# Second product terms: exchanged by plain transfers and added on GpSimd, in place of accumulating transfers

## The chip, the cores and the metric

The kernel runs on one core of a Trainium2 chip. The metric is device time in microseconds (us) for one execution, the smaller the better. A core has engines that run side by side, each its own list of instructions in order: TensorE (PE, with its weight loads shown apart as PEld), VectorE (DVE), ScalarE (ACT), GpSimd (POOL) and SyncE (SP), whose work here is to issue transfers. Transfers (DMA) run on 16 shared DMA engines, from queues of their own: one is filled by SP, another by POOL.

## The reference

Two state-space convolutions of the same input are mixed by a gate. Input `u` is 2048 positions by 512 channels, the state has 128 terms for each channel:

```python
dt = jnp.exp(log_dt)
A = -jnp.exp(log_A_real) + 1j * A_imag
C = (C_real + 1j * C_imag) * dt[:, None]
P = jnp.exp((A * dt[:, None])[:, :, None] * pos[None, None, :])
K = 2.0 * jnp.einsum("dn,dnl->dl", C, P).real
y = jnp.fft.irfft(jnp.fft.rfft(u_t, 2 * L) * jnp.fft.rfft(K, 2 * L), 2 * L)[:, :, :L]
...
g = _sigmoid((x * gate_w).sum(-1, keepdims=True))
return g * a + (1 - g) * b        # a, b: y + u * D_skip with the weights A and B
```

## The kernel before

**Stages.** Parameters come in eight chunks of 128 channel rows and are prepared in five batches (`prep_ops`; the first on DVE, the other four on POOL, 25 steps each there). Each chunk is eight units, 64 in all. For one unit POOL multiplies two decay grids out of small bases (`grid0` writes 128x1024 numbers, `grid1` 128x512, both line 530), PE makes phases (`phase`), ACT turns them into sines and cosines, DVE multiplies them into the grids, and PE contracts the result into the convolution kernel's samples (`modes`, line 581). The grids have two buffers each, so POOL can run about two units ahead of `modes`. Four units make a block; there are 16.

**The transform of a block.** Kernel samples and inputs are transformed in two steps on PE (`first`, line 603; `s2`, line 640). The complex product of the two spectra is taken on DVE by `products` (line 651), which writes two terms: the first into the block's part of the tile `xall` (`xk(b)`; two such parts are used by turns), the second into `t2`, another part of `xall`, of which there is one. Real and imaginary parts lie on different halves of the 128 partitions, and the second term comes out on the opposite half. So the second has to cross over before the two can be summed. For 15 of the blocks `add_products` (line 681) does both at once: POOL issues four accumulating transfers per block, for two halves `h` of the columns and two halves `x` of the partitions, 256 KB each. `inverse` (line 694) then reads the sum on PE, its first two groups the columns of `h = 0`, its last two those of `h = 1`. For the last block no sum is made: `inverse` multiplies the second term by `mt`, which is the matrix `mi` with its row halves exchanged. `keep_z` stores the result; after every fourth block `final` multiplies by the gated synthesis matrix and `final_keep` and `final_out` write out.

**What sets the order.** All operations are listed in program order and then emitted in the order of the list `ORDER`; every engine keeps this order exactly, and so does SP's list of transfers. An instruction that must wait holds up everything behind it on its engine. `SLOTS` gives each PSUM tile one of eight banks.

**Tiles that the change touches.** `ks` (samples of a unit, four buffers), `ot` (outputs, four buffers), `mt`, `ident` (the identity; used by warm-up matmuls, by the preparation and by `hold`, idle filler matmuls) and `f1` (the smaller grid with its product).

Of the kernel before, what the change touches and what calls it, by code (L numbers as in the profile page):

```python
# [19 lines left out]
M = 32  # L20
# [185 lines left out]
def tile_gated_s4d(ctx: ExitStack, tc: tile.TileContext, nsb, a, out):  # L206
# [629 lines left out]
    def block(b):  # L836
# [9 lines left out]
        if 0 <= b < nblk - 1:  # L846
            for h in range(2):
                for x in range(2):
                    op("ya", add_products, b, h, x)
# [172 lines left out]
```

## Time and profile before

| | |
|---|---|
| Time, median of 3 runs (lowest, highest) | 500.42 us (500.07, 506.3) |
| The profiled execution: its own time | 500.83 us |
| its span, first to last instruction | 498.9 us |
| mean granted TensorE clock | 0.983 |
| busy in the span: PE, ACT, DVE, POOL | 443.1, 405.2, 392.9, 332.9 us |
| packets of SP's queue (q1) | 27360, 31.41 MB, 22.2% of 16 engines |
| packets of POOL's queue (q0) | 4800, 15.73 MB, 19.0% of 16 engines |

Busy time of an engine is the union of its instructions' spans; "idle before" is what an engine stood still ahead of an instruction, with the event that ended it. Matmuls are pipelined, so a busy PE isn't PE at its best.

### The profile page before, as it was taken

The page shows a single profiled execution, that of the slowest core. Times are in us where ns is not written, and L with a number is a line of the kernel's source. Part 1 is how long each engine was busy: PE and PEld are TensorE (multiplying, and loading weights), DVE is VectorE, ACT ScalarE, POOL GpSimd, SP SyncE. Part 2 cuts the span into 40 slices and gives each one's busy share as a digit, 9 for nine tenths or more (in the row PEclk, how much of TensorE's full clock was granted, in tenths as well). Part 3 has the DMA queues.
Part 4 walks back from the last instruction along what each step waited for, and adds up shares of the span by engine and source line. Part 5 has one row for each costly group of instructions (what it writes and reads, how often), then busy time and mean ns, then how long its engine had stood idle before and what let it go on. Part 6 is the DMA issues. An engine that isn't in the chain of part 4 may idle for free.

```text
span 498.9 us, 27908 instructions
## 1 busy us (share of the span) xinstructions
PE 443.1 (89%) x12448; PEld 357.4 (72%) x12448; DVE 392.9 (79%) x864; ACT 405.2 (81%) x816; POOL 332.9 (67%) x316
## 2 busy tenths in 40 slices
PE   5967997988999887997999898978998899989988
PEld 5855556876778675875888686767777779767984
DVE  6394898899999975888889795787999898976402
ACT  5697999989899987788998997777999797964323
POOL 1497998899997977686667866385775754862000
PEclk9998999999999999998999998999999999999999
DMA  4669705316550704246430744134443733174201
GB/s 143 226 235 287 186 11 126 69 25 123 136 94 12 150 27 98 69 77 157 79 61 11 150 105 74 57 78 96 113 77 60 157 65 67 36 169 74 59 25 60
DMA packets 32279, 48.92 MB, mean 98 GB/s; under 512 B 10144, under 2 KB 17440, under 8 KB 32160
## 3 DMA queue, kind: packets, MB, share of 16 engines
q1 hardware_dynamic: 27360, 31.41, 22.2%
q0 software_dynamic: 4800, 15.73, 19.0%
q8 instruction: 97, 1.59, 1.3%
q14 instruction: 22, 0.18, 0.1%
HBM read 17.25 MB, written 5.77 MB: 46 GB/s over the span
## 4 chain that ended last, share of the span: by engine, by line
PE 61%; ACT 12%; DVE 8%; issue 8%; POOL 7%; DMA 5%; SPq 0%; DVEq 0%; ACTq 0%; POOLq 0%
PE ps L640 15%; PE psi L694 11%; PE pk L581 9%; PE p0s L514 7%; PE ps L603 5%; DMA xall<-xall 5%; PE pf L718 4%; POOL f L530 3%; PE psu L603 3%; ACT bas L498 2%; ACT xall L610 2%; PE pw L289 2%; PE pw L293 2%; PE psg L782 1%; DVE xall L651 1%
## 5 line engine op out<-in xcount | busy, mean ns | idle before, releaser
L530 POOL TENSOR_TENSOR f<-bas 128x1024 f32<-128x1024 f32 (+1 forms) x128 | 207.7, 1689 | 78.6 <-PE pk L581 45.4
L640 PE MATMUL ps<-xall,gk 128*64 128x64 f32 (+1 forms) x1728 | 111.3, 251 | 5.7 <-DVE f L553 1.7
L640 PEld LDWEIGHTS ps<-xall,gk 128*64 128x64 f32 (+1 forms) x1728 | 101.4, 153 | 19.1 <-issue 2.7
L651 DVE TENSOR_TENSOR xall<-ps,v 128x256 f32<-128x256 f32 x256 | 94.5, 415 | 15.5 <-PE ps L640 13.4
L581 PE MATMUL pk<-f,f 128*32 128x64 f32 x4096 | 74.3, 223 | 15.5 <-issue 7.2
L581 PEld LDWEIGHTS pk<-f,f 128*32 128x32 f32 x4096 | 62.9, 111 | 27.6 <-issue 17.2
L694 PE MATMUL psi<-mi,xall 128*128 128x128 f32 x512 | 71.8, 287 | 4.4 <-issue 2.7
L681 POOL DMA_DIRECT2D xall<-xall x60 | 60.1, 1152 | 17.4 <-DVE f L557 8.1
L694 PEld LDWEIGHTS psi<-mi,xall 128*128 128x128 f32 x512 | 63.5, 196 | 10.2 <-issue 5.0
L557 DVE TENSOR_TENSOR f<-f,p0c 128x512 f32<-128x512 f32 x64 | 43.6, 682 | 14.4 <-ACT p0c L526 13.8
L514 PE MATMUL p1s<-cph,ones 64*128 64x512 f16 x128 | 49.3, 386 | 3.2 <-DVE ks L591 2.1
L553 DVE TENSOR_TENSOR f<-f,p0c 128x512 f32<-128x512 f32 x64 | 43.6, 681 | 8.6 <-ACT p0c L526 7.9
L603 PEld LDWEIGHTS ps<-w,ks 64*64 64x64 f32 x2048 | 35.4, 140 | 20.7 <-issue 7.7
L514 PE MATMUL p0s<-cph,ones 64*128 64x512 f16 x128 | 49.4, 386 | 0.5 <-ACT xall L610 0.4
L514 PE MATMUL p1s<-cph,rot 64*128 64x512 f16 x128 | 49.0, 382 | 0.8 <-issue 0.8
L569 DVE TENSOR_TENSOR f<-f,p1c 128x512 f32<-128x512 f32 x64 | 43.6, 682 | 7.3 <-ACT p1c L526 5.6
L610 ACT COPY xall<-ps 128x512 f32<-128x512 f32 x64 | 36.9, 612 | 15.0 <-PE ps L603 15.0
L603 PE MATMUL ps<-w,ks 64*64 64x64 f32 x2048 | 40.3, 227 | 9.6 <-issue 6.3
L514 PE MATMUL p0s<-cph,rot 64*128 64x512 f16 x128 | 48.9, 382 | 0.0
L701 ACT COPY z<-psi 128x512 f32<-128x512 f32 x64 | 37.9, 609 | 12.7 <-PE psi L694 12.7
L573 DVE TENSOR_TENSOR f<-f,p1s 128x512 f32<-128x512 f32 x64 | 43.6, 681 | 5.2 <-ACT p1s L523 4.1
L565 DVE SCALAR_TENSOR_TENSOR f<-f,p0s 128x512 f32<-128x512 f32 x64 | 43.4, 680 | 3.2 <-ACT p0s L523 3.0
(128 smaller groups left out, 824.1 us busy)
## 6 DMA issues: line engine op xcount, KB each, us to landing
xall<-xall POOLq DMA_DIRECT2D x60, 256.0 KB, 5.2
v<-v SPq DMA_DIRECT2D x64, 128.0 KB, 3.3
uraw<-in_us SPq DMA_DIRECT2D x16, 256.0 KB, 3.8
z<-in_ut SPq DMA_DIRECT2D x16, 256.0 KB, 6.4
out_dram<-ot SPq DMA_DIRECT2D x28, 128.0 KB, 2.2
par<-in_par SPq DMA_DIRECT2D x8, 256.0 KB, 4.4
gk<-in_gk SPq DMA_DIRECT2D x4, 512.0 KB, 6.1
eg<-in_eg SPq DMA_DIRECT2D x4, 512.0 KB, 5.6
```

Source lines behind the costliest of these rows:

```text
L514: PE.matmul(ps, w[h : h + 64], cph[h : h + 64, j], start=j == 0, stop=j == 3, tile_position=(h, 0))
L530: G.tensor_tensor(o.rearrange("p k (a b) -> p k a b", b=8), x[:, :, hi : hi + n].unsqueeze(3).to_broadcast([128, 16, n, 8]), x[:, :, lo : ...
L553: V.tensor_tensor(f0[:, 0, :, 0:32], f0[:, 1, :, 0:32], half(u, p0c[u], True), OP.mult)
L557: V.tensor_tensor(f0[:, 0, :, 32:64], f0[:, 1, :, 32:64], half(u, p0c[u], False), OP.mult)
L569: V.tensor_tensor(f[:, 0], f[:, 1], p1c[u], OP.mult)
L581: PE.matmul(pk[32 * kd : 32 * kd + 32, i, :], f1[:, p, 4 * i + kd, :], f0[:, p, 4 * i + kd, :], start=p == 1, stop=p == 0, tile_position=( ...
L603: PE.matmul(ps[h][64 * ri : 64 * ri + 64, n, :], x[r], w1[r, ri, r], start=True, stop=True, tile_position=(64 * h, 64 * ri),)
L610: S.copy(o, pxs[key][h])
L640: PE.matmul(ps[h : h + w, j, 0:n], gk[:, k, h : h + w], xall[:, x0:x1, 2 * k : 2 * k + 2], start=True, stop=True, tile_position=(0, h),)
L651: V.tensor_tensor(k.rearrange("p x (k t) -> p k x t", t=2), p2s[b, g][:, :, 0:64].rearrange("p k (x t) -> p k x t", t=2), vv.unsqueeze(3). ...
L681: G.dma_start(out=xk(b)[o, s], in_=t2[t, s], accum_op=OP.add)
L694: PE.matmul(ps[:, i, :], t[:, x : x + 2, :].rearrange("p x k -> p (x k)"), w, start=n == 0, stop=n == len(parts) - 1,)
```

## The change

The accumulating transfers go. For each block but the last and each column half, `exchange` has SP issue two plain transfers that copy the second term into the new tile `tx` with the partition halves exchanged, and `add_products` has POOL add `tx` to `xk(b)` in one 128x1024 instruction. `tx` has one buffer and holds one column half: the second half's exchange waits for the first half's add. That is 60 transfers of 256 KB on SP and 30 additions on POOL, for 60 transfers on POOL.

Room for `tx` (4 KB of each partition) comes from `mt` (its content is loaded over `ident` late in the run), from `ks` (three buffers, not four) and from `ot` (two, not four); the last outputs are gathered in a buffer of `f1`.

`ORDER` and `SLOTS` are new lists. On PE the units come in the same sequence with nearly the same work between them from unit 10 to unit 40; in the first units the gate matmuls (`ga`) stand earlier. On SP twelve, not three, of the 16 loads of `ut` stand ahead of the first load of `rot` (`turns`). On POOL the preparation of the third batch done there stands earlier. Counted in the two lists, after the memsets at the start POOL has this to do up to the last grid of unit 19, that grid included:

| | before | changed |
|---|---|---|
| grids | 40 | 40 |
| `amplitudes` | 3 | 3 |
| preparation steps (batches 1, 2, 3) | 25 + 25 + 8 | 25 + 25 + 23 |
| transfers issued | 12 | 0 |
| additions | 0 | 6 |

The fifteen additional preparation steps are nine TENSOR_TENSOR (128x256), five TENSOR_SCALAR (128x256) and one TENSOR_TENSOR of 128x768 (`rest`, line 406).

```diff
--- before.py
+++ after.py
@@ -31,173 +31,175 @@
 
 
 ORDER = [
...
 ]
 
 
 SLOTS = [
     int(c) for c in (
...
     )
 ]
 
@@ -238,10 +240,10 @@
     gk = const.tile([128, M, 128], F32, name="gk")
     dl = const.tile([128, 4 * nunit], F32, name="dl")
     mi = const.tile([128, 128], F32, name="mi")
-    mt = const.tile([128, 128], F32, name="mt")
     v = const.tile([128, 4, M, 32], F32, name="v")
     xall = const.tile([128, 128, 2 * M], F32, name="xall")
     t2 = xall[:, 32:64]
+    tx = const.tile([128, 16, 2 * M], F32, name="tx")
     z = const.tile([128, 128, 5 * NB], F32, name="z")
     eg = const.tile([128, 2, Q, M], F32, name="eg")
     warm = const.tile([128, 1], F32, name="warm")
@@ -584,7 +586,7 @@
                     )
 
     def keep(u):
-        kss[u] = work.tile([128, 4, Q], F32, name="ks", tag="ks", bufs=4)
+        kss[u] = work.tile([128, 4, Q], F32, name="ks", tag="ks", bufs=3)
         S.copy(kss[u], pks[u])
 
     def skip(u):
@@ -675,21 +677,26 @@
     def both_v(i, h):
         dma(v_at(hi, i, 0, h), v_at(lo, i, 0, h))
 
-    def add_products(b, h, x):
+
+    def exchange(b, h, x):
         o, t = slice(64 * x, 64 * x + 64), slice(64 - 64 * x, 128 - 64 * x)
-        s = slice(16 * h, 16 * h + 16)
-        G.dma_start(out=xk(b)[o, s], in_=t2[t, s], accum_op=OP.add)
+        dma(tx[o], t2[t, 16 * h : 16 * h + 16])
+
+    def add_products(b, h):
+        x = xk(b)[:, 16 * h : 16 * h + 16]
+        G.tensor_tensor(x, x, tx, OP.add)
 
     def z_place(b):
         sb, j = divmod(b, 4)
         return j if sb % 2 == 0 else 4 - j
+
 
 
     def inverse(b, g):
         pis[b, g] = ps = bank("psi", (128, 4, 128))
         for i in range(4):
             x = 2 * (4 * g + i)
-            parts = [(xk(b), mi), (t2, mt)] if b == nblk - 1 else [(xk(b), mi)]
+            parts = [(xk(b), mi), (t2, ident)] if b == nblk - 1 else [(xk(b), mi)]
             for n, (t, w) in enumerate(parts):
                 PE.matmul(
                     ps[:, i, :], t[:, x : x + 2, :].rearrange("p x k -> p (x k)"), w,
@@ -728,7 +735,7 @@
         return o[128 * i : 128 * (i + w)].rearrange("(p c) -> p c", p=128)
 
     def final_keep(sb, j, dp):
-        ots[sb, j, dp] = work.tile([128, 256], F32, name="ot", tag="ot", bufs=4)
+        ots[sb, j, dp] = work.tile([128, 256], F32, name="ot", tag="ot", bufs=2)
         w = 128 if sb == nsb - 1 else 256
         S.copy(ots[sb, j, dp][:, 0:w], pfs[sb, j, dp].rearrange("p a b -> p (a b)"))
 
@@ -755,7 +762,10 @@
         pfs[i] = ps
 
     def last_keep(i, dp):
-        ots[i, dp] = work.tile([128, 256], F32, name="ot", tag="ot", bufs=4)
+        if dp == 0:
+            f = work.tile([128, 2, 16, M], F32, name="f1", tag="f1").rearrange("p v k m -> p (v k m)")
+            for n in range(2):
+                ots[i, n] = f[:, 256 * n : 256 * n + 256]
         o = ots[i, dp].rearrange("p (a b) -> p a b", a=8)
         copy = V.tensor_copy if dp else S.copy
         for rq in range(4):
@@ -846,7 +856,8 @@
         if 0 <= b < nblk - 1:
             for h in range(2):
                 for x in range(2):
-                    op("ya", add_products, b, h, x)
+                    op("ya", exchange, b, h, x)
+                op("yb", add_products, b, h)
         if nxt:
             for h in range(2):
                 for i in range(2):
@@ -874,8 +885,6 @@
         op("ga", gate, j)
         op("gs", gate_sig, j)
         op("ge", gate_e, j)
-    for h in range(2):
-        op("lm", dma, mt[64 * h : 64 * h + 64], a["mi"][64 - 64 * h : 128 - 64 * h])
     for u in range(nunit):
         if u % 8 == 0:
             c = u // 8
@@ -885,6 +894,9 @@
                         batch(i)
                 chunk(c + 1)
         unit(u)
+        if u == nunit - 8:
+            for h in range(2):
+                op("lm", dma, ident[64 * h : 64 * h + 64], a["mi"][64 - 64 * h : 128 - 64 * h])
         b, n = divmod(u, 4)
         if b % 2 and n < 2 and b < nblk - 1:
             inputs(b + 1 + n)
```

More of the change, by code (lines that the diff above doesn't have):

```diff
@@ L192 @@
     int(c) for c in (
-        "012313131203231045671056710432305410726067134215247362064051571203517501406340652137625304"
-        "751046016231460173537512043672106723744160516743241726052657234605714531705426025471251746"
-        "301604352435041670362145125460173165726074265310253014215640372157146752350275604135231457"
-        "602670425352130264725065316205374134621357662074275436120162032176456204573134150261230572"
-        "546617045704521643125275071243624712341213246540752653121460154712543761016451675403142204"
-        "152637625074310775210471257625142675073320167540215437563412743145065260431773167502704512"
-        "726375607132164501754231762073463147065414140525417052461351276306740563130206314275140761"
-        "35064257370215170173041673152454325745314123521515"
+        "012312120131120450627642701246423670631452613672013260543146720564507350127350231657416307"
+        "243571206702557614306412641537014753624270641235412745670540346752617462754301570436324076"
+        "542140624057362167520143040153327612540341325062735026507561201437271403164257412630612304"
+        "275257147531056725436425017450261353640761532047162761325762732614056124132734620750265130"
+        "437621364310425640721024307271562156735267215420341475621465105730415652061052725130643163"
+        "245230471625402613402637415376412674012346013205273546104502617310247357531266050457364021"
+        "326045061475302315064760520617374026135012435676521241345705742645210363260540767524031452"
+        "60724043254757317135137562652741617232375112572171"
     )
```

310 rows, old and new, of the table ORDER are left out of this document.

## Prediction, made before the changed kernel was run

> **What bounds the kernel now.** I read the page first: which engine is full, and when.
>
> ```profile
> span 498.9 us, 27908 instructions
> ...
> PE 443.1 (89%) x12448; PEld 357.4 (72%) x12448; DVE 392.9 (79%) x864; ACT 405.2 (81%) x816; POOL 332.9 (67%) x316
> ...
> PE   5967997988999887997999898978998899989988
> ...
> POOL 1497998899997977686667866385775754862000
> ```
>
> PE has 89% of the span, so 55.8 us of it is idle and no change that leaves the matmuls alone can gain more than that. POOL looks harmless at 67%, but its row of slices is near full from the third to the twelfth and loose behind it. So the share has to be split by stage. The windows below run from the first base (18 us) to the end of unit 19's grids (154), from there to the end of unit 26's (206), and on to the last grid (448). Columns: length, then busy us (and instructions) of each engine, granted clock, DMA share, GB/s.
>
> ```profile
> core 0: us, PE busy (x) PEld busy (x) DVE busy (x) ACT busy (x) POOL busy (x), PEclk, DMA share, GB/s
> 18.00:154.00 136.00, 118.56 (x2800) 89.31 (x2800) 115.44 (x229) 126.39 (x245) 125.39 (x123) 0.97 0.51 132
> 154.00:206.00 52.00, 44.62 (x1270) 36.61 (x1271) 41.05 (x89) 45.49 (x88) 38.55 (x37) 0.97 0.35 70
> 206.00:448.00 242.00, 221.76 (x6755) 181.65 (x6739) 206.67 (x450) 206.75 (x429) 163.99 (x148) 0.99 0.43 89
> ```
>
> There are two regimes. Up to 154 us POOL is busy 125.4 of 136 us (92%), ACT 126.4 (93%), PE only 118.6 (87%): the grids and the preparation on POOL pace the units. From 206 us on PE is busy 92% and POOL 68%: PE paces, and POOL waits for buffers. What the change adds to POOL therefore costs in the first stage and is free in the last. The view of waits of POOL in the first window says how much room it has:
>
> ```profile
> engine line waited for: us in total, times, longest us
> POOL bas L501 <- DVE dec L435: 16.1, 1, 16.1
> POOL mx L390 <- ACT axy L386: 3.2, 1, 3.2
> POOL bas L503 <- ACT bas L498: 2.2, 2, 1.5
> POOL f L530 <- issue: 1.2, 1, 1.2
> POOL f L530 <- ACT bas L498: 0.7, 1, 0.7
> ...
> POOL f L530 <- PE pk L581: 0.3, 1, 0.3
> ```
>
> The 16.1 us lie ahead of the window. Inside it POOL waited 0.3 us for PE to free a grid: it is not held back by PE there, PE follows it.
>
> **What the change removes and adds on POOL.** Prices, from the groups of instructions by form (busy us, mean ns, idle before) and from POOL's timeline (start, length, with x2 where two are merged):
>
> ```profile
> L530 POOL TENSOR_TENSOR f<-bas 128x1024 f32<-128x1024 f32 x64 | 133.8, 2097 | 52.2 <-PE pk L581 23.9 <-DVE v L665 7.0 <-DVE f L569 4.8
> ...
> L681 POOL DMA_DIRECT2D xall<-xall x60 | 60.1, 1152 | 17.4 <-DVE f L557 8.1 <-PE psu L603 3.3 <-PE pf L718 1.2
> ...
> L394 POOL TENSOR_SCALAR tb<-tb 128x256 f32<-128x256 f32 x12 | 12.4, 1032 | 0.7
> ...
> L390 POOL TENSOR_TENSOR tb<-tb,sg 128x256 f32<-128x256 f32 x12 | 8.8, 730 | 0.4
> ...
> L406 POOL TENSOR_TENSOR tb<-tb,sp 128x768 f32<-128x768 f32 x3 | 5.6, 1879 | 0.0
> ```
> ```profile
> 115.38 1.71 POOL L681 DMA_DIRECT2D xall<-xall  x2
> 116.54 3.56 POOL L530 TENSOR_TENSOR f<-bas 128x512 f32<-128x512 f32 x2
> 119.47 1.43 POOL L681 DMA_DIRECT2D xall<-xall  x1
> 120.06 1.95 POOL L530 TENSOR_TENSOR f<-bas 128x512 f32<-128x512 f32 x1
> ```
>
> An issue of an accumulating transfer is recorded with 1152 ns, but two of them start at 115.38 and the next instruction at 116.54, and the one at 119.47 is followed at 120.06: POOL moves on after 0.59 us, and the records overlap. So a removed issue returns 0.59 us, not 1.15 (the two ends). An addition of 128x1024 has no row. Two-operand instructions took 0.730 us at 256 columns and 1.879 at 768, that is 1.149 for 512 columns, so 1024 come to 2.45 us (an estimate by that line). Bounds: 2.10, the grid of that size, whose operands are broadcast, and 2.51, the 768 row scaled up. I take 2.45, since both operands are full.
>
> The Trainium skill ("GPSIMD Engine Reference", section "Engine selection") speaks against such an addition on this engine: two-operand elementwise work is about twice as slow there as on VectorE. Its 4497 ns for 2048 columns (section 3.1) would make 2.25 us for 1024, an estimate from that page; by it the sum below would be 1.2 us smaller.
>
> Over the whole run that is 30 x 2.45 - 60 x 0.59 = 38 us more on POOL. In the first stage it is, up to the last grid of unit 19, by the counts of the two order lists: 6 additions (14.7 us) for 12 issues (7.1 us), and fifteen more preparation steps of the third batch: 9 x 0.730 + 5 x 1.032 + 1.879 = 13.6 us. Net 21.2 us. POOL's work in the window becomes 125.4 + 21.2 = 146.6 us in 136: unit 19's grids come 10.6 us late even if POOL never stands still, 21.2 us late if it stands still as long as before. Of its 10.6 us idle I leave 4 in place (bases and angles that come from ACT, 6.1 us above): 15 us late.
>
> Behind that the kernel can catch up only where PE and ACT have room. In 154 to 206 PE is idle 7.4 us and ACT 6.5; I take 4 of it. From 206 on I take nothing: PE is at 92% and its sequence of units is nearly unchanged. POOL's other 24 additions (59 us, less 48 issues at 0.59, 28 us) fall where it has 91.5 us idle (13.45 and 78.0 in the two later windows): nothing. If that cover were gone, they would cost up to 31 us.
>
> **The transfers.** Rows of issues (KB, median us from issue to landing) and of the accumulating line:
>
> ```profile
> xall<-xall POOLq DMA_DIRECT2D x60, 256.0 KB, 5.2
> v<-v SPq DMA_DIRECT2D x64, 128.0 KB, 3.3
> uraw<-in_us SPq DMA_DIRECT2D x16, 256.0 KB, 3.8
> ...
> out_dram<-ot SPq DMA_DIRECT2D x28, 128.0 KB, 2.2
> ```
> ```profile
> who waited for it (us, times):
>   DVE xall L651: 1.8, 2
>   PE psi L694: 1.7, 3
> ...
> DMA to landing us min/median/max: 3.4/5.2/8.2
> ```
>
> A plain exchange of 256 KB has no row; 3.3 (half the size, same kind) and 5.2 bound it, I take 3.8. One buffer `tx` makes a chain per block: 2 x (3.8 + 2.45) = 12.5 us from products to the last sum, where four accumulating transfers, issued 0.59 apart, took 3 x 0.59 + 5.2 = 7.0. The 5.5 us lie beside four units of other PE work, and `inverse` and the next `products` stand late enough in the lists that before they waited 3.5 us in all. I put 0 on it; without cover it is 5.5 us in each of 15 blocks. Late next would be the next block's products, since `t2` is read until the second exchange has landed.
>
> On SP 60 issues are added, each behind the products and the addition ahead of it. Whoever stands behind them, input loads, copies of `v`, reloads of `rot` and outputs, waits too. With two `ot` buffers `final_keep` may wait 2.2 us for the output two ahead; with three `ks` buffers `keep` may wait for `first`. I put 0 to 2 us on these, value 0.
>
> **Sum.** 500.8 (the profiled execution's own time; 498.9 span and 1.9 around it; 0.4 above the median) + 15 - 4 + 0 = 512 us. Its own range: 10.6 late and 6.5 caught up is 505; 21.2 late and nothing caught up is 522.
>
> **Rivals.** Faster, by the start. The new lists put gate matmuls and the `ut` loads earlier, where PE stands still:
>
> ```profile
> 0.00:62.00 62.00, 47.82 (x1010) 37.15 (x1010) 40.62 (x106) 48.43 (x90) 39.56 (x47) 0.97 0.70 216
> ```
>
> PE is idle 14.2 us there. Were that all won and POOL's early preparation done in waits, the time would be 500.8 - 14.2 = 487. For it: the gates fill those gaps. Against: up to unit 6 the same matmuls come in both lists, and the grids that they wait for come from POOL, which is loaded more. It decides if unit 6 is contracted earlier than before.
>
> No change: POOL's lead of two units absorbs it, because ACT was at 93% in the first stage and sets the pace itself. Then the time is 500 to 505, or 497 if the 3.5 us of waits for accumulating transfers go too. The Trainium skill ("SBUF — State Buffer", section "SBUF: two separate sides") has a rule for the latter: transfers issued by GpSimd are starved when VectorE locks a port that they share, those issued by SyncE never are. The spread from 3.4 to 8.2 us would fit it, but only 3.5 us were lost to it, within 2% of the time.
>
> Slower still, by order on the queues. SP already stood long behind single waits:
>
> ```profile
> SPq L256 <- ACT ot L733: 96.2, 11, 20.3
> SPq L256 <- DVE v L665: 90.5, 10, 25.2
> ```
>
> If an exchange is stuck behind such a wait, its addition blocks POOL, and with it the grids. Ten of thirty additions at 2 us more, beyond POOL's lead, give 512 + 20 = 532. Against it: from 206 us POOL has slack.
>
> **Numbers.** The likeliest case, 505 to 522, gets 0.55, a quarter of it under 2% (510.4); no change 0.14; faster 0.17; slower still 0.14. Two per cent is about what a measurement of this kernel can tell from no change. Faster by over 2%: 0.17. Within: 0.14 + 0.14 = 0.28. Slower: 0.41 + 0.14 = 0.55. The range, 488 to 528, leaves out most of the faster case and the upper half of the slowest.
>
> **What would show it.** Right: in the profile of the changed kernel POOL is over 97% busy up to unit 19's grids, these end 10 to 20 us later than 154, additions take 2.1 to 2.5 us, and from then on the units keep the old distance. Wrong: unit 19's grids at 154 or earlier; additions under 2 us or idle for long ahead of them; waits of PE or DVE for `tx` and `xall` above 5 us; or a loss that grows after 206 us.

## The result, and the profile after

The change made the kernel slower: 518.73 us median (516.43 to 519.22, 4 runs) against 503.08 us for the kernel before (500.07 to 506.3, 4 runs), a ratio of 1.0301 with a 95% interval from 1.0212 to 1.039. The profiled execution took 518.71 us, its span is 516.6 us against 498.9.

The page of the changed kernel, first its span and shares, then the rows of slices of PE and POOL:

```profile
span 516.6 us, 27950 instructions
...
PE 449.7 (87%) x12448; PEld 359.1 (70%) x12448; DVE 396.1 (77%) x864; ACT 408.3 (79%) x817; POOL 351.3 (68%) x286
...
PE   5979687798798898998789898878999989989896
...
POOL 0499999899998597967565776838574856580300
```

POOL's busy time rose from 332.9 to 351.3 us. PE's rose only by 6.6 us, so 11 of the 17.7 us are new idle time of PE. The same three windows as before, of the changed kernel (length, busy us and instructions of each engine, granted clock, DMA share, GB/s):

```profile
18.00:154.00 136.00, 112.70 (x2587) 82.03 (x2582) 108.91 (x215) 118.19 (x225) 129.22 (x124) 0.92 0.41 115
154.00:206.00 52.00, 46.31 (x1285) 37.88 (x1276) 45.22 (x98) 48.82 (x95) 40.78 (x32) 1.00 0.32 73
206.00:448.00 242.00, 219.45 (x6472) 177.56 (x6472) 201.65 (x434) 203.39 (x419) 161.42 (x118) 1.00 0.34 83
```

In the first, POOL is busier (129.2 us, 95%) and PE does 5.9 us less. In the last, PE does less too, 219.5 for 221.8 us, at a slightly better clock (1.00 for 0.99): something holds it there as well. The new groups of instructions and the new transfer, from the page:

```profile
L687 POOL TENSOR_TENSOR xall<-xall,tx 128x1024 f32<-128x1024 f32 x30 | 71.6, 2388 | 56.6 <-DMA tx<-xall 45.8
...
L701 PE MATMUL psi<-mi,xall 128*128 128x128 f32 x512 | 72.8, 289 | 8.1 <-POOL xall L687 7.9
...
tx<-xall SPq DMA_DIRECT2D x60, 256.0 KB, 3.9
```

An addition takes 2.39 us, an exchange 3.9 us from issue to landing. The new thing is the middle column: POOL stood still 45.8 us until an exchange had landed. The list of waits gives the number of times and the longest (us in total, times, longest):

```profile
POOL xall L687 <- DMA tx<-xall: 45.8, 12, 12.5
...
PEld psi L701 <- POOL xall L687: 12.5, 11, 2.2
...
PE psi L701 <- POOL xall L687: 7.9, 10, 1.9
```

One of the twelve is block 8. VectorE's timeline, SyncE's queue and POOL's timeline at that place (start, length, instruction, idle before it):

```profile
309.34 1.41 DVE L653 TENSOR_TENSOR xall<-ps,v 128x256 f32<-128x256 f32 x4
```
```profile
310.82 8.88 SPq L258 DMA_DIRECT2D tx<-xall  x4
```
```profile
309.17 1.95 POOL L532 TENSOR_TENSOR f<-bas 128x1024 f32<-128x1024 f32 x1 [2.92 <-issue]
315.42 2.34 POOL L687 TENSOR_TENSOR xall<-xall,tx 128x1024 f32<-128x1024 f32 x1 [4.30 <-DMA tx<-xall]
317.73 1.06 POOL L532 TENSOR_TENSOR f<-bas 128x512 f32<-128x512 f32 x1
```

The products end at 310.75 and SyncE issues the exchange at once, at 310.82. POOL ended its grid at 311.12, just in time for the products, and then stands 4.30 us for the transfer. The grid behind the addition starts at 317.73: 6.9 us after the exchange was issued.

The ends of grids, from the trace, show where the time is lost. Later than in the kernel before, in us (the rows below "after" are the experiments' kernels, told in the next section):

| Kernel | unit 8 | unit 19 | unit 30 | unit 48 | unit 63 | span |
|---|---|---|---|---|---|---|
| after | 10.0 | 15.0 | 9.1 | 6.5 | 14.6 | 17.7 |
| noexch | 9.3 | 12.6 | 5.4 | -3.1 | 2.2 | 1.2 |
| noadd | 8.4 | 4.6 | 0.4 | -8.4 | -1.7 | 2.8 |
| tinyexch | 9.3 | 12.7 | 5.3 | -3.6 | 2.3 | 2.6 |
| tinyadd | 8.0 | 6.6 | 1.0 | -8.0 | -0.6 | 1.4 |
| tosum | 9.5 | 14.5 | 9.4 | 5.5 | 15.5 | 20.0 |
| late | 11.0 | 19.8 | 19.0 | 17.7 | 27.5 | 29.1 |
| addlater | 7.3 | 12.2 | 7.2 | 9.0 | 22.3 | 26.3 |

(Unit 48's grids stand earlier among their surroundings in the new list: in noexch they come 3 us early where the unit's skip term comes 7 us late. That column compares kernels with the new order among themselves.) The first addition starts at 91.5 us. Unit 7's grids end before that, at 85.3 us, and are 9.1 us late: the additions have no part in it. POOL's list says where it may come from: not only the third batch of preparation stands earlier in the new list, the first two do so as well. Up to the last grid of unit 8 POOL has run 52 preparation instructions, for 36 in the kernel before. It isn't the fifteen steps of the third batch: in late, where these are back at their old places, unit 8 is 11.0 us late.

### The profile page after: what moved, and what is told of

It reads as the page before. It is cut to its first block, busy times and chain, and to the rows that moved or that the text cites. A ratio compares the mean times of both kernels' runs of the same rounds, so it can differ in the third digit from the quotient of the medians.

```text
span 516.6 us, 27950 instructions
## 1 busy us (share of the span) xinstructions
PE 449.7 (87%) x12448; PEld 359.1 (70%) x12448; DVE 396.1 (77%) x864; ACT 408.3 (79%) x817; POOL 351.3 (68%) x286
## 5 line engine op out<-in xcount | busy, mean ns | idle before, releaser
L532 POOL TENSOR_TENSOR f<-bas 128x512 f32<-128x512 f32 (+1 forms) x128 | 191.6, 1514 | 50.8 <-issue 17.6
L642 PE MATMUL ps<-xall,gk 128*64 128x64 f32 (+1 forms) x1728 | 113.2, 252 | 6.7 <-DMA gk<-in_gk 1.7
L687 POOL TENSOR_TENSOR xall<-xall,tx 128x1024 f32<-128x1024 f32 x30 | 71.6, 2388 | 56.6 <-DMA tx<-xall 45.8
L583 PE MATMUL pk<-f,f 128*32 128x64 f32 x4096 | 72.8, 222 | 22.9 <-issue 6.2
L583 PEld LDWEIGHTS pk<-f,f 128*32 128x32 f32 x4096 | 62.3, 111 | 34.9 <-issue 14.5
L701 PEld LDWEIGHTS psi<-mi,xall 128*128 128x128 f32 x512 | 63.9, 197 | 17.5 <-POOL xall L687 12.5
L559 DVE TENSOR_TENSOR f<-f,p0c 128x512 f32<-128x512 f32 x64 | 43.6, 681 | 15.7 <-ACT p0c L528 10.8
L522 ACT ACTIVATE p0c<-p0s 128x512 f32<-128x512 f32 x64 | 38.4, 600 | 11.7 <-DVE ks L593 6.7
L563 DVE TENSOR_TENSOR f<-f,p0s 128x512 f32<-128x512 f32 x64 | 43.7, 682 | 1.5 <-ACT p0s L525 0.7
```

Source lines behind the costliest of these rows:

```text
L532: G.tensor_tensor(o.rearrange("p k (a b) -> p k a b", b=8), x[:, :, hi : hi + n].unsqueeze(3).to_broadcast([128, 16, n, 8]), x[:, :, lo : ...
L559: V.tensor_tensor(f0[:, 0, :, 32:64], f0[:, 1, :, 32:64], half(u, p0c[u], False), OP.mult)
L563: V.tensor_tensor(o, o, half(u, p0s[u], True), OP.mult)
L583: PE.matmul(pk[32 * kd : 32 * kd + 32, i, :], f1[:, p, 4 * i + kd, :], f0[:, p, 4 * i + kd, :], start=p == 1, stop=p == 0, tile_position=( ...
L642: PE.matmul(ps[h : h + w, j, 0:n], gk[:, k, h : h + w], xall[:, x0:x1, 2 * k : 2 * k + 2], start=True, stop=True, tile_position=(0, h),)
L687: G.tensor_tensor(x, x, tx, OP.add)
```

## The experiments

Ratios are to the kernel before, run on the same chip beside each group, 502.7 to 504.6 us.

**late.** The preparation of the third and fourth batches on POOL goes back to its old places in the order.

```diff
 ORDER: (pp0..pp34 of batches 3 and 4, lp, al) behind the same grids as in the kernel before
```

> The changed kernel with one part of its order undone: the preparation steps of the third and fourth batch on GpSimd stand where the order of before has them (behind the same grids), everything else as in the changed kernel. Theory (work of GpSimd up to unit 19's grids paces the kernel): 13.6 us of work leave that stretch, so unit 19's grids end near 158 us, not 168.8, and the time falls by 7 to 11 us, to 508 to 512. Rival (waits for the exchange, behind SyncE's and GpSimd's order, are the cause): nothing changes before unit 19's grids but the filling, the time stays at 516 to 520. Rival (the first 20 us cost it): 516 to 520 too, with units 2 to 8 still 9 us late.

Measured: 529.21 us, ratio 1.0526 (1.0479 to 1.0572). The theory fell, and the time is above both rivals too: the kernel became 10 us slower, not faster. In its first window POOL works only 112.5 of 136 us, and unit 19's grids still come 19.8 us late. POOL stands instead, for the most part until PE or VectorE lets it write a grid (POOL's waits between 84 and 180 us):

```profile
POOL f L503 <- PE pk L554: 8.5, 3, 6.9
...
POOL f L503 <- DVE xall L624: 4.5, 1, 4.5
...
POOL xall L658 <- DMA tx<-xall: 3.0, 2, 2.6
```

So the fifteen earlier steps had filled time in which POOL would have stood still, or their later place holds up something else; the run doesn't tell the two apart. Its share of busy time in that window doesn't show what sets the pace.

**noadd** and **noexch** leave out one half of the mechanism each: no addition (the exchanges remain; second terms are missing), or no exchange (`tx` is cleared once; the additions remain).

```diff
     def add_products(b, h):
-        x = xk(b)[:, 16 * h : 16 * h + 16]
-        G.tensor_tensor(x, x, tx, OP.add)
+        pass
...
     def exchange(b, h, x):
-        o, t = slice(64 * x, 64 * x + 64), slice(64 - 64 * x, 128 - 64 * x)
-        dma(tx[o], t2[t, 16 * h : 16 * h + 16])
+        pass
```

> The changed kernel without the 30 additions on GpSimd: the exchange transfers stay, the second terms of 15 blocks are left out of the sum. Theory (work on GpSimd): 14.3 us less up to unit 19's grids and no wait for tx anywhere; the time falls by 10 to 15 us, to 504 to 509. Rival (the order's early preparation and start are the whole cause): 514 to 519. Rival (the load of the transfers on the DMA engines or on SyncE's queue): 514 to 519.

> The changed kernel without the 60 exchange transfers: tx is cleared once and the 30 additions stay, so the second terms of 15 blocks are left out of the sum. Theory (work on GpSimd): up to unit 19's grids GpSimd waited 1.5 us for tx, so these move by 2 us at most; the waits for tx behind that (45.8 us, 12 times) lie in slack; the time falls by 0 to 5 us, to 514 to 519. Rival (waits for the exchange are the cause): 500 to 506.

Measured: noadd 504.38 us, ratio 1.0028 (0.9999 to 1.0057), as its theory had it; noexch 503.41 us, ratio 1.0008 (0.9974 to 1.0041), where its theory fell and its rival came. Either half alone is free; only both together cost about 15 us. Nor is it the order, the fewer buffers or the clock: noexch keeps the whole order and the buffers and ran at a mean granted clock of 0.970, the changed kernel at 0.968. POOL does the same additions in noexch, and unit 19's grids are 12.6 us late as well, but the lag is made up behind it: 5.4 us at unit 30, 2.2 at unit 63. Its last window has 8.8 us more PE work than the changed kernel's:

```profile
206.00:448.00 242.00, 228.20 (x6835) 183.98 (x6826) 210.01 (x454) 212.06 (x440) 169.63 (x121) 1.00 0.19 49
```

**accum, accum2 and mech** were to separate the mechanism from the order. accum has the accumulating transfers, issued by POOL, at the places of the exchanges in the new order; accum2 has them at the places of the additions; mech has exchanges and additions in the order of before.

```diff
     def exchange(b, h, x):      # accum; in accum2 both are issued in add_products
         o, t = slice(64 * x, 64 * x + 64), slice(64 - 64 * x, 128 - 64 * x)
-        dma(tx[o], t2[t, 16 * h : 16 * h + 16])
+        s = slice(16 * h, 16 * h + 16)
+        G.dma_start(out=xk(b)[o, s], in_=t2[t, s], accum_op=OP.add)
...
     def add_products(b, h):
-        x = xk(b)[:, 16 * h : 16 * h + 16]
-        G.tensor_tensor(x, x, tx, OP.add)
+        pass                    # accum
...
 ORDER of before: yb(b, 0) ahead of iv(b, 0), ya(b, 1, x) behind it, yb(b, 1) ahead of iv(b, 2)   # mech
```

> The changed kernel, its order and banks kept, with the accumulating transfers of before issued by GpSimd where the exchange was issued, and no additions. Theory (work on GpSimd in the first stage): six additions at 2.39 us go and twelve issues at 0.59 us come, 7.3 us less up to unit 19's grids, which end near 162 us; the time falls by 6 to 11 us, to 508 to 513. Rival (the order found is the cause, whatever sums the terms): 516 to 520. Rival (the exchange and its waits are the whole cause): 500 to 505.

> The changed kernel's order, with the accumulating transfers of the kernel before: GpSimd issues both of a half at the place where the changed kernel adds, the exchanges by SyncE and the additions are gone. This is the clean undo of the mechanism inside the new order. Theory (the mechanism costs, the new order alone does not): 500 to 507 us. Rival (the new order itself costs): 510 to 518 us.

> The kernel before's order with the mechanism of the change: the exchanges of a block's first half stand where its first accumulating transfer stood, the addition directly ahead of the first inverse that reads it, the second half's exchanges behind that addition, its addition directly ahead of the third inverse; result transfers directly behind their copies, since there are fewer buffers for them. Theory (the dependent chain of exchange and addition costs, in any order): 512 to 530 us, more than 10 us above the kernel before. Rival (the changed kernel's order is the cause): 499 to 507 us.

Measured: accum 568.08 us, ratio 1.1309 (1.1254 to 1.1363); accum2 614.50, ratio 1.2211 (1.2141 to 1.2282); mech 578.24, ratio 1.1474 (1.1404 to 1.1544). All three are inconclusive on the question. In accum some first terms are written behind the transfer and replace the sum; in accum2 and mech some transfers of a block's second half stand behind the next block's products, which have overwritten `t2`. They therefore wait for work that neither kernel makes them wait for. accum2's waits show it (57.6 us of PE for the sums), and so do mech's:

```profile
PE psi L673 <- DMA xall<-xall: 57.6, 14, 6.9
```
```profile
PEld psi L672 <- POOL xall L658: 70.4, 23, 7.2
...
PE psi L672 <- POOL xall L658: 64.8, 21, 7.0
```

What they do show is that a mechanism and a list that was not made for it don't go together. The mechanism's cost inside the old order stays open.

**tosum.** The addition writes its result into `tx`; POOL waits and works as before, but PE's inverse no longer waits for the sum.

```diff
-        G.tensor_tensor(x, x, tx, OP.add)
+        G.tensor_tensor(tx, x, tx, OP.add)
```

> The changed kernel, but each addition writes its result into tx itself and not into xall. GpSimd still waits for the exchange at the same places and spends the same time adding; what is gone is that the inverse products (PE) wait for the sum. The second product terms are left out of the output. Theory: what costs the time is that GpSimd stands in line for the exchange with the grids of later units behind it; then this takes 514 to 519 us, as the changed kernel, and GpSimd's wait for the exchange stays near 46 us. Rival: the wait of PE's inverse for the sum (20 us in the changed kernel's list of waits) is what costs; then 502 to 507 us. If both count: 508 to 513.

Measured: 518.64 us, ratio 1.0311 (1.0254 to 1.0368), the time of the changed kernel. (The list puts 37.8 us of POOL's idle time down to the exchange, not 46.) PE's 20 us of waits for the sum (12.5 of its weight loads, 7.9 of its matmuls) cost nothing; the loss comes through POOL or through the transfers behind it.

**dveadd.** The additions go to VectorE, at the same places.

```diff
-        G.tensor_tensor(x, x, tx, OP.add)
+        V.tensor_tensor(x, x, tx, OP.add)
```

> The changed kernel with the thirty additions on VectorE at the same places of the order. GpSimd loses 71.6 us of additions and the 46 us that it stood in line for the exchange. An addition of 128x1024 is taken at 1.2 us on VectorE, an estimate from a VectorE operation of the same shape in the trace of before. Theory (GpSimd's line is what costs): unit 19's grids come within 5 us of the kernel before, and the time is 498 to 507 us. Rival (the chain transfer, addition, inverse costs wherever the addition stands, since VectorE then stands in line with the skip terms and products behind it): 512 to 525 us.

Measured: 555.91 us, ratio 1.1051 (1.0974 to 1.1128), worse than either case. An addition took 1.27 us there (median), and VectorE stood still only 19.1 us for exchanges, but POOL, 71.6 us lighter, now stands 108.3 us until PE frees a grid:

```profile
POOL f L503 <- PE pk L554: 108.3, 31, 12.6
...
DVE xall L658 <- DMA tx<-xall: 19.1, 8, 4.8
```

Unit 19's grids came 15.6 us late, where the theory had 5 at most. A likely reason, which no run tests, is what stands behind the addition on VectorE: the products of sines and grids that PE needs next. VectorE also has 38 us more to do (30 x 1.27).

**addlater.** In seven blocks the first addition, and what must follow it, moves behind POOL's next grids.

```diff
 ORDER: yb(b, 0) behind the next g0 or g1 for b = 3, 5, 6, 7, 8, 10, 12; ya(b, 1, x) behind yb(b, 0)
```

> The changed kernel with the first-half addition of seven blocks (3, 5, 6, 7, 8, 10, 12) moved behind the next grids step of GpSimd (about 2 us of work; two steps in block 10), and the second half's exchanges behind it where they stood earlier. These seven additions waited 2.1 to 7.6 us each for their exchange in the changed kernel, 31.2 us in all. Theory (the loss is GpSimd standing in line for the exchange with grids behind it): GpSimd's wait for the exchange falls from 45.8 to 20 to 30 us and the time to 508 to 515 us. Rival (the loss goes with the chain transfer, addition, second transfer, addition as a whole, so that a later addition only makes the second half later): 516 to 524 us.

Measured: 530.31 us, ratio 1.0538 (1.0482 to 1.0594), above both cases. The wait fell even a little further than expected, from 45.8 to 18.9 us, and the time rose by some 11 us. What was a wait for the exchange is now a wait for PE, up from 16.9 us, and VectorE waits for the later second exchange, up from 0.8:

```profile
POOL f L503 <- PE pk L554: 37.2, 8, 10.8
POOL xall L658 <- DMA tx<-xall: 18.9, 6, 14.2
...
DVE xall L624 <- DMA tx<-xall: 13.3, 4, 9.6
```

This speaks against a price of the idle time by itself, and for one of how late all that hangs on the addition comes.

**freeadd.** The addition reads the second terms where they lie, so that it doesn't depend on the exchange.

```diff
-        G.tensor_tensor(x, x, tx, OP.add)
+        G.tensor_tensor(x, x, t2[:, 16 * h : 16 * h + 16], OP.add)
```

> The changed kernel with all sixty exchanges issued and all thirty additions made, but each addition takes its second operand from the second product terms where they lie and not from tx, so that it does not depend on the exchange; the output has the terms of the wrong halves. Work of GpSimd and transfers are all there; only the wait of the addition for the exchange, and that of the next exchange for the addition, are gone. Theory (the wait alone costs): 499 to 506 us. Rival (transfers beside the additions slow each other, or SyncE's queue does it): 512 to 519 us.

Measured: 533.18 us, ratio 1.0578 (1.0512 to 1.0645). It doesn't decide: the edit puts new dependencies in the place of the old. POOL waits for VectorE's products 35.9 us, and the next block's products, which overwrite `t2`, now wait for the addition:

```profile
POOL xall L658 <- DVE xall L624: 35.9, 10, 7.1
...
DVE xall L624 <- POOL xall L658: 13.8, 7, 2.7
```

Its rival, that transfers and additions slow each other, is answered by noadd and noexch: an exchange lands in 3.7 us (median) without additions, 3.9 with them, and an addition takes 2.37 us (median) with the exchanges and without.

**tinyadd** and **tinyexch** keep every wait and every place, and shorten one link each to a sixteenth of its data. The other fifteen sixteenths of the second terms are left out.

```diff
-        G.tensor_tensor(x, x, tx, OP.add)
+        G.tensor_tensor(x[:, 0], x[:, 0], tx[:, 0], OP.add)
...
-        dma(tx[o], t2[t, 16 * h : 16 * h + 16])
+        dma(tx[o, 0], t2[t, 16 * h])
```

> The changed kernel with each addition cut to one of its sixteen rows (128x64 in place of 128x1024): GpSimd still waits for both exchanges at the same places, and the second half's exchanges still wait for the addition, but nearly all of the 71.6 us of additions is gone. Fifteen sixteenths of the second product terms are left out. Theory (GpSimd's wait for the exchange, with the grids behind it, carries the loss, not the work of adding): 512 to 519 us. Rival (the time of the addition, on GpSimd or in the chain, carries it): 501 to 507 us. If each has a part: 507 to 512.

> The changed kernel with each exchange cut to one of its sixteen rows (16 KB in place of 256 KB), tx cleared once; waits and additions are all there. Fifteen sixteenths of the second product terms are left out. Theory (the wait costs by its length): the transfer lands faster than the 3.9 us of the changed kernel, I estimate at 2 to 2.8 us from the 3.0 us of the 128 KB result transfers, the wait for it falls from 45.8 to 25 to 40 us, and the time to 505 to 514 us. Rival (the tie between the queues costs, not its length, or the bytes do not set the landing): 515 to 520 us.

Measured: tinyadd 503.78 us, ratio 0.9977 (0.9947 to 1.0007); tinyexch 503.98 us, ratio 1.0001 (0.9969 to 1.0033). Either one takes back the whole loss: in tinyadd the theory fell and the rival came, in tinyexch the time is just under the theory's range. The instructions on `tx` in tinyadd (min, median, max ns) and what ended POOL's idle time ahead of them:

```profile
L658 POOL TENSOR_TENSOR xall<-xall,tx x30: 313/319/331, 91.6 to 468.5; 128x64 f32<-128x64 f32 x30
its engine sat idle before it (us, times) until:
  DMA tx<-xall: 44.4, 10
```

The same in tinyexch, with the landing:

```profile
L659 POOL TENSOR_TENSOR xall<-xall,tx x30: 2348/2371/2552, 90.9 to 469.5; 128x1024 f32<-128x1024 f32 x30
...
  DMA tx<-xall: 24.5, 7
...
DMA to landing us min/median/max: 1.6/2.8/3.8
```

tinyadd is the telling one: POOL stands for exchanges as long as in the changed kernel, 44.4 against 45.8 us, and nothing is lost. (Of these, 20.5 and 17.8 us lie ahead of block 14's additions, which have no grid behind them. Ahead of the other 28 additions POOL stands still 44.7 us in tinyadd and 38.8 in the changed kernel, all waits counted.) What differs is that the grid behind starts 2.1 us earlier. Block 8 once more, tinyadd's and then tinyexch's timeline of POOL:

```profile
301.83 0.32 POOL L658 TENSOR_TENSOR xall<-xall,tx 128x64 f32<-128x64 f32 x1 [4.25 <-DMA tx<-xall]
302.11 1.07 POOL L503 TENSOR_TENSOR f<-bas 128x512 f32<-128x512 f32 x1
```
```profile
307.42 2.36 POOL L659 TENSOR_TENSOR xall<-xall,tx 128x1024 f32<-128x1024 f32 x1 [2.15 <-DMA tx<-xall]
309.73 1.08 POOL L504 TENSOR_TENSOR f<-bas 128x512 f32<-128x512 f32 x1
```

Their exchanges were issued at 297.28 and 304.95, as SyncE's queue shows:

```profile
297.28 6.00 SPq L229 DMA_DIRECT2D tx<-xall  x4
```
```profile
304.95 5.95 SPq L229 DMA_DIRECT2D tx<-xall  x4
```

From the issue to the next grid it is 4.8 us in both, where the changed kernel takes 6.9. That grid is unit 40's. Against tinyexch the changed kernel is 5.9 us late at unit 39 and 8.0 at unit 40, and it doesn't get these 2 us back: here the order has room for 4.8 us and not for 6.9. (tinyadd also frees POOL of 62 us of work, but noexch, with all of it, is as fast; tinyexch also moves less, but noadd, with whole exchanges, is as fast.) At the units of the table tinyexch's grids end within 0.5 us of noexch's: below this length, little more is to be won. The room isn't the same in every block. For the first halves of the first fourteen blocks, with those in which POOL comes late anyhow, the medians from the issue to POOL's next instruction are 7.8 us in the changed kernel, 5.9 in tinyadd and 6.9 in tinyexch; for the second halves they are 10.6, 8.8 and 11.0, so there a long chain costs tinyexch nothing. Against tinyexch the changed kernel is only 0.7 to 0.8 us late up to unit 18; from unit 19 on it loses 11.5 us up to unit 63, in steps that come at most of the blocks, and 2.8 us in the tail.

How late grids cost time shows in VectorE's waits for them, over the whole run, in the changed kernel and then in tinyexch:

```profile
DVE f L571 <- POOL f L532: 7.3, 7, 2.9
...
DVE f L559 <- POOL f L532: 4.6, 3, 2.1
...
DVE f L555 <- POOL f L532: 3.1, 5, 1.2
```
```profile
DVE f L531 <- POOL f L504: 3.1, 4, 1.4
...
DVE f L543 <- POOL f L504: 2.7, 5, 1.0
...
DVE f L527 <- POOL f L504: 0.6, 2, 0.3
```

That is 15.0 us against 6.4; it is 5.0 us in noexch, 1.0 in tinyadd, and 15.7 in tosum, which is as slow as the changed kernel. For an exchange VectorE waits 0.8 us in the changed kernel.

## Why the prediction was right and wrong

The time came out 6.7 us above the forecast of 512, inside the range; the distance to the kernel before is 15.65 us, where the forecast had 11. But two steps were wrong and nearly made each other good.

**POOL's work in the first stage: the number right, in part by luck.** Unit 19's grids were forecast 15 us late and came 15.0 us late. The sum behind it was 146.6 us of work and 4 of idle time; measured, up to that grid, it is 142.5 and 8.3 (the window's length, then busy times, as above):

```profile
18.00:168.80 150.80, 125.86 (x2847) 92.92 (x2839) 120.76 (x241) 132.03 (x252) 142.46 (x133) 0.93 0.39 108
```

The additions were priced well, at 2.45 us each, and took 2.39. The preparation grew by 11.5 us, not 13.6, and the twelve issues that went had taken 9.0 us, not 7.1: in the kernel before an issue took POOL, up to the start of its next instruction, 0.60 us in the median but 0.76 in the mean, since some took up to 1.7. (Over the whole run POOL's busy time rose by 18.4 us, where 38 were forecast.) The idle time that the forecast took for filled came back elsewhere, 4.3 us of it, and that made up for the work that was missing. The mechanism is borne out for the additions: without them (noadd) unit 19 is 10.4 us less late. For the fifteen preparation steps no run shows it; late takes them out of the stage and its unit 19 comes later still. The sign in the profile was over 97% busy time; it was 95%, and late, at 83%, shows that this share was no measure of the delay.

The Trainium skill ("GPSIMD Engine Reference", section "Engine selection") has two-operand work on GpSimd about twice as slow as on VectorE; 2388 ns here and 1274 ns in dveadd agree, 1.9 times. The 2.25 us that the prediction estimated from that page's 2048 columns were 6% short.

**"In 154 to 206 ... I take 4 of it": right.** Of 15.0 us at unit 19, 11.7 are left at unit 26, whose grids end at 218.1 us for 206.4; so 3.3 were caught up.

**"From 206 on I take nothing: PE is at 92%": wrong.** This step carried the 11 us of loss that the forecast ended with. Where nothing else holds PE, the lag is made up: noexch goes from 12.6 us at unit 19 to 2.2 at unit 63, with 228.2 us of PE work in the last 242, 94%. The early work of POOL, 17 us more of it by the profile, is in the end worth nothing measurable (a ratio of 1.0008). Eight per cent of idle time over 242 us were 20 us of room.

**"The 5.5 us lie beside four units of other PE work ... I put 0 on it": wrong.** The sizes were right (3.9 us for an exchange where 3.8 was taken), the cover was not. The step asked who waits for the sum, PE's inverse and the next products, and for PE rightly found room; tosum confirms that this wait costs nothing. It did not ask what stands behind the waiting addition on POOL: the grids of later units. (One of the rivals did, below.) The price is what tinyexch takes back, a ratio of 1.0001 for 1.0301, so 15 us, or 1 us for each of the 15 blocks: between the ends given, 0 and 5.5.

**The 0 us for SP's added issues and the fewer buffers: right.** noadd has the 60 issues, both it and noexch have the buffers, and neither lost time.

**"POOL's other 24 additions ... fall where it has 91.5 us idle: nothing": right as work, and not as a place.** In noexch they cost nothing. But idle time in a window says only that there is room somewhere; the addition can't use it before its exchange has landed.

**The rival "slower still, by order on the queues"** had the mechanism by half: an addition that waits does block POOL and with it the grids. Its cause was mostly another. The one long wait of this kind is block 6's: of its first exchange's two transfers the second stood on SyncE's queue until 257.66, behind a result transfer; SyncE's queue and then POOL's timeline:

```profile
252.43 0.58 SPq L258 DMA_DIRECT2D tx<-xall  x1
257.27 0.34 SPq L258 DMA_DIRECT2D out_dram<-ot  x1
257.66 0.46 SPq L258 DMA_DIRECT2D tx<-xall  x1
```
```profile
260.70 2.36 POOL L687 TENSOR_TENSOR xall<-xall,tx 128x1024 f32<-128x1024 f32 x1 [7.57 <-DMA tx<-xall]
```

In blocks 4, 9 and 11 a second transfer left 2.2 to 4.0 us behind the first as well, but POOL stood at most 1.6 us ahead of the addition there. In most other places, as in block 8, the exchange left at once and the wait was its own flight.

**Faster** and **no change** did not come. The start was no gain: unit 7 was 9.1 us late before any addition had run. Of the prediction's own signs of being wrong three showed: idle time ahead of the additions (56.6 us in all), waits of PE for the sum above 5 us, and a loss that grows after 206 us (11.7 us at unit 26, 14.6 at unit 63).

**What stays open.** That the grids behind the addition carry the loss is supported by tosum, tinyadd and tinyexch, but the second exchange, which waits for the first addition, gets earlier along with them in the last two, and no run separates the two. The waits speak for the grids: VectorE stood 8.6 us longer for them than in tinyexch, and only 0.8 us for an exchange. But 8.6 us are not the whole 15, and the rest isn't traced. Nor is it shown which part of the new order makes the first units late. Two `tx` buffers, which would separate the grids from the second exchange, need another 4 KB of each partition and were not tried. No version tried beats the kernel before; the variants at 503 to 504 us leave terms out.

## What to carry to other kernels

Where a dependent step is put on an in-order engine, price it by the time at which the instruction behind it can start: the producer's end, the transfer's landing and the step itself, against the moment at which the order needs that next instruction. In the block followed here 4.8 us were free and 6.9 were not. Idle time ahead of the step is no price: some 44 us of it stood in a kernel that lost nothing and in one that lost 15 us. And before a stage is called full because its engine is busy 92% of it, look whether the rest, summed over the stage, is larger than the delay that it is to absorb.

## What the runs showed of the hardware that was not expected

A sixteenth of the bytes (256 B for 4 KB in each of 64 partitions) made an exchange land in 2.8 us, not 3.9 (medians): some 2.7 us of it do not depend on the size, if the rest is taken as proportional (1.1 us for fifteen sixteenths, so 1.2 for all). By this estimate shrinking saves at most 1.2 us of such a transfer; here 1.1 us were enough to take the loss back.
